# Block loads and VectorE block transposes for q and k, and w_in kept once in DRAM, in a fused attention, MoE and soft-MoE kernel

## The chip, the cores and the metric

The kernel runs on one core of one Trainium2 chip. The metric is the device time of one execution in microseconds. Three executions of the kernel before took 681.17, 681.69 and 682.29 us: a median of 681.69 us.

## The reference, cut to what matters

Three layers follow one another. q, k and v are float32 with 4 batches, 12 heads, 448 rows and 64 columns. The weights w_in and w_out come in as float64.

```python
scores = scale * np.matmul(q, k.transpose(0, 1, 3, 2))
scores = np.where(mask, -1000000000.0, scores)
attn = softmax(scores)
x = np.matmul(attn, v)                     # -> (4*448, 768)
h = x @ w_in                               # 768 -> 2048
g = h * np.clip(h + 3.0, 0.0, 6.0) / 6.0
x = g @ w_out                              # 2048 -> 768
logits = x @ phi                           # 32 slots
slot_input = softmax(logits, axis=0).T @ x
slot_out[e] = np.maximum(slot_input[e] @ w1[e], 0.0) @ w2[e]   # 8 experts
out = softmax(logits, axis=1) @ slot_out
```

## The kernel before, in words

**The stages.** The heads of a batch are taken in pairs, so there are 24 pairs (`attention(i)`, `i` from 0 to 23), six to a batch. After the six pairs of a batch come its 16 units of the middle layer (`ft` from 0 to 15), each a product of 128 columns of w_in with the 448 tokens of the batch. The units of one batch run between the pairs of the next, so that pairs and units alternate from the end of batch 0 on. After the last unit of batch 3 come the expert stage and the output, which stream w1 and w2 (named `in_moe_w_dram` in the profile, into `ring` tiles) from DRAM.

**The order of the work.** `Schedule` is a planner that runs when the kernel is built. Each step has an engine (or a choice of engines), a cost, the steps that it depends on, the buffers that it uses and a due time. `run` places the steps one after the other and so writes out the order of every engine's queue; the numbers in `TU` are its due times and weights. It decides, too, which engine takes a step that has a choice, and puts in filler matmuls (L385) where it sees TensorE idle. On the chip every engine then works through its own queue in that order and waits where an operand isn't there. All DMAs are issued on one queue, SP's (`dma`, L401).

**q and k of a pair.** Two DMAs each bring q and k into `qr` and `kr` (one buffer each) with 112 rows to a partition group. Four TensorE transposes each (L434) turn them into a PSUM tile `t`, of which there are two, shared with the units. ScalarE copies the tile into the first half of `qp` or `kp` (L404), rounded to fp32r, and VectorE subtracts that from the tile for the second half (L440). Products are then made of the three larger terms of (hi + lo) times (hi + lo). The scores are made first with hi alone (L457) in two halves that share one PSUM tile `ps`, VectorE takes the row maxima of each half (L472, L476), POOL or VectorE makes a diagonal matrix of them (L486 to L490), TensorE makes the transposed scores less the maxima (L507, L512), ScalarE the exponentials (L522), POOL cuts them at the diagonal (L530), in two steps, and TensorE multiplies by v (L545). The result is normalised (L556 to L558), turned (L566) and split into hi and lo (L404, L574) as `xp`.

**w_in of a unit.** The float64 bits of w_in are turned into float32 on the chip in batch 0 (`conv`, L587 to L599) and land in one of two `cx` tiles. That float32 tile is stored to DRAM as `wf_d`, split into hi and lo (ScalarE L682, VectorE L685 or POOL L687) in one of two `wpl` tiles, and the split pair is stored, too, as `wi_d`. Batches 1 and 2 load the split pair (768 KB) straight into `wpl`; batch 3 loads the float32 tile (384 KB) into `cx` and splits it again. A unit is 18 matmuls of 448 columns (L701), then L706 and L708 make g, four transposes (L715) turn it, and ScalarE stores it (L720, L722).

```python
if b == 0 or fin:                                       # L681: split on the chip
    e = sc.add("ACT", 0.84, ...)                        # L682
    wr = sc.any([("DVE", 1.0, ...), ("POOL", 2.0, ...)], [e], [cx, w], ps_)
elif not fin:                                           # L693: load the split pair
    wr = sc.load(0.79e6, ...dma(w.t.bitcast(F32), wi_d[ft])...)
```

## Time and profile before

| what | value |
|---|---|
| time, median of three | 681.69 us |
| time of the profiled execution | 680.19 us |
| its span | 678.4 us |
| PEld (weight loads, beside the matmuls) | 478.2 us, 70% |
| DVE (VectorE) | 329.7 us, 49% |
| ACT (ScalarE) | 261.4 us, 39% |
| POOL (GpSimd) | 96.5 us, 14% |
| DMA | 161.56 MB, 72.9% of 16 engines |
| granted clock of TensorE, mean | 0.956 |

The span is the time from the first to the last instruction of the profiled execution; some 1.8 us of its time lie around it. PE is the matmul side of TensorE. Busy shares are means over stages that differ: the first stage is attention of batch 0 beside the conversion of w_out, the middle ones are units and pairs, and the last is a stream of weights. The table of stretches among the rows below keeps them apart.

### The profile page before, as it was taken

The page shows a single profiled execution, that of the slowest core. Times are in us where ns is not written, and L with a number is a line of the kernel's source. Part 1 is how long each engine was busy: PE and PEld are TensorE (multiplying, and loading weights), DVE is VectorE, ACT ScalarE, POOL GpSimd, SP SyncE. Part 2 cuts the span into 40 slices and gives each one's busy share as a digit, 9 for nine tenths or more (in the row PEclk, how much of TensorE's full clock was granted, in tenths as well). Part 3 has the DMA queues.
Part 4 walks back from the last instruction along what each step waited for, and adds up shares of the span by engine and source line. Part 5 has one row for each costly group of instructions (what it writes and reads, how often), then busy time and mean ns, then how long its engine had stood idle before and what let it go on. Part 6 is the DMA issues. An engine that isn't in the chain of part 4 may idle for free.

```text
span 678.4 us, 15815 instructions
## 1 busy us (share of the span) xinstructions
PE 628.4 (93%) x6556; PEld 478.2 (70%) x6556; DVE 329.7 (49%) x814; ACT 261.4 (39%) x488; POOL 96.5 (14%) x197
## 2 busy tenths in 40 slices
PE   8798989999999999999999999999999999977474
PEld 6677868787888778888888688888698843522133
DVE  6886978888784534444335554323433333101101
ACT  2575566544544433323334332334344322201011
POOL 1332332325340011110001001000000000000000
PEclk7998999999999999999999999999999999996666
DMA  8989899989979833555445343335962399999997
GB/s 205 312 293 297 270 262 335 338 236 333 298 267 361 264 89 122 157 159 138 141 142 168 91 135 124 124 135 212 370 239 93 117 341 385 378 373 357 331 313 220
DMA packets 142615, 161.56 MB, mean 238 GB/s; under 512 B 71632, under 2 KB 113872, under 8 KB 142544
## 3 DMA queue, kind: packets, MB, share of 16 engines
q1 hardware_dynamic: 142544, 160.56, 72.9%
q8 instruction: 51, 0.84, 0.5%
q14 instruction: 20, 0.16, 0.1%
HBM read 129.86 MB, written 30.67 MB: 237 GB/s over the span
## 4 chain that ended last, share of the span: by engine, by line
PE 68%; DMA 13%; DVE 9%; SPq 3%; issue 2%; ACT 2%; POOL 0%; DVEq 0%; ACTq 0%; POOLq 0%
PE ph L701 19%; PE pl L701 13%; DMA ring<-in_moe_w_dram 7%; PE ps L507 5%; PE t L715 5%; DVE ps L472 4%; DMA raw<-in_moe_w_out_dram 3%; PE o L545 3%; SPq L401 3%; PE t L566 3%; PE ps L457 2%; PE t L434 2%; PE t L859 2%; PE ps L1025 2%; PE ph L730 2%
## 5 line engine op out<-in xcount | busy, mean ns | idle before, releaser
L701 PE MATMUL ph<-xp,wpl 128*128 128x448 f32 x720 | 157.0, 371 | 0.0
L701 PEld LDWEIGHTS ph<-xp,wpl 128*128 128x128 f32 x720 | 132.2, 188 | 15.2 <-ACT r L706 2.2
L701 PE MATMUL pl<-xp,wpl 128*128 128x448 f32 x432 | 94.2, 371 | 0.0
L701 PEld LDWEIGHTS pl<-xp,wpl 128*128 128x128 f32 x432 | 79.4, 188 | 9.0 <-issue 2.6
L472 DVE CUSTOM_DVE_ANT_0 ps<-ps,maskw 128x448 f32<-128x448 f32 (+3 forms) x144 | 61.7, 429 | 48.5 <-PE ps L457 38.6
L530 POOL TENSOR_SCALAR_AFFINE_SELECT s<-s 128x256 f32<-128x256 f32 x96 | 43.6, 478 | 232.9 <-ACT s L522 141.5
L706 ACT ACTIVATE r<-ph,three 128x448 f32<-128x448 f32 x40 | 25.5, 637 | 102.5 <-PE ph L701 102.5
L507 PE MATMUL ps<-qp,kp 64*64 64x64 f32 (+3 forms) x576 | 57.5, 306 | 3.8 <-ACT s L522 3.8
L522 ACT ACTIVATE s<-ps 128x896 f32<-128x896 f32 (+2 forms) x72 | 50.3, 734 | 25.9 <-PE ps L512 22.0
L708 DVE SCALAR_TENSOR_TENSOR g<-r,ph 128x448 f32<-128x448 f32 x40 | 24.7, 618 | 62.9 <-ACT r L706 62.9
L507 PEld LDWEIGHTS ps<-qp,kp 64*128 64x128 f32 (+1 forms) x576 | 42.1, 175 | 17.7 <-issue 6.6
L545 PE MATMUL o<-vr,s 128*64 128x65 f32 (+1 forms) x1536 | 53.6, 224 | 0.0
L545 PEld LDWEIGHTS o<-vr,s 128*64 128x64 f32 (+1 forms) x1536 | 48.6, 137 | 5.8 <-issue 3.8
L587 ACT ACTIVATE ca<-raw 128x768 f32<-128x768 f32 x32 | 29.3, 917 | 29.7 <-DMA raw<-in_moe_w_out_dram 10.0
L708 DVE SCALAR_TENSOR_TENSOR g<-r,pl 128x448 f32<-128x448 f32 x24 | 14.8, 617 | 50.8 <-ACT r L706 50.8
L720 ACT ACTIVATE gtok<-t 128x384 f32<-128x384 f32 x64 | 31.2, 487 | 19.2 <-PE t L715 19.0
L715 PE MATMUL t<-ident,g 128*128 128x128 f32 (+1 forms) x256 | 37.9, 279 | 0.2 <-DVE g L708 0.2
L706 ACT ACTIVATE r<-pl,three 128x448 f32<-128x448 f32 x24 | 15.3, 636 | 58.3 <-PE pl L701 58.3
L596 DVE SCALAR_TENSOR_TENSOR cw<-ca,cw 128x768 uint32<-128x768 uint32 x32 | 32.9, 1029 | 3.4 <-ACT ca L587 1.7
L1123 PE MATMUL o<-ring,wos 128*32 128x384 f32 (+1 forms) x256 | 22.5, 474 | 11.8 <-DMA ring<-in_moe_w_dram 11.8
L715 PEld LDWEIGHTS t<-ident,g 128*128 128x128 f32 (+1 forms) x256 | 26.9, 133 | 6.1 <-issue 1.5
L457 PE MATMUL ps<-kp,qp 64*128 64x448 f32 (+1 forms) x192 | 27.3, 344 | 4.1 <-DVE mc L472 3.0
(209 smaller groups left out, 827.1 us busy)
## 6 DMA issues: line engine op xcount, KB each, us to landing
ring<-in_moe_w_dram SPq DMA_DIRECT2D x45, 768.0 KB, 11.6
wpl<-wi_d SPq DMA_DIRECT2D x32, 768.0 KB, 4.2
raw<-in_moe_w_out_dram SPq DMA_DIRECT2D x16, 768.0 KB, 6.1
raw<-in_moe_w_in_dram SPq DMA_DIRECT2D x16, 768.0 KB, 7.4
wi_d<-wpl SPq DMA_DIRECT2D x16, 768.0 KB, 6.1
ring<-in_moe_w_dram SPq DMA_DIRECT2D x21, 512.0 KB, 8.0
wo_d<-gtok SPq DMA_DIRECT2D x16, 384.0 KB, 4.1
wf_d<-cx SPq DMA_DIRECT2D x16, 384.0 KB, 7.5
```

The lines of the kernel that those rows point to most:

```text
L457: nc.tensor.matmul(ps.t[:n, h, c:c + w], pl["q"].t[r, 0, q0:q0 + n], pl["k"].t[r, 0, 0:w], start=(t == part[0][0]), stop=adds, skip_group_ ...
L472: nc.vector.tensor_tensor_reduce(out=x, in0=x, in1=maskw[:n, 320 - q0:320 + n] if t else maskw[:n, 320:320 + n], scale=-1.0, scalar=3.0e38 ...
L507: nc.tensor.matmul(ps.t[:kn, h, col:col + n], pl["k"].t[r, x, q0:q0 + kn], pl["q"].t[r, y, q0:S], start=(c == 0 and col == 0), stop=False, ...
L522: nc.scalar.activation(out=o, in_=x, func=ACTF.Exp, scale=SCALE)
L530: nc.gpsimd.affine_select(out=x, in_=x, pattern=[[0, 2], [1, kn]], compare_op=ALU.is_ge, fill=0.0, base=0, channel_multiplier=-1)
L545: nc.tensor.matmul(o.t[64 * h:64 * h + 64, VD * j:VD * j + VD], s.t[:kn, h, c:c + 64], vr.t[:kn, h, t, :], start=(t == 0), stop=(t == ts[- ...
L596: e = sc.add("DVE", 1.04, lambda: nc.vector.scalar_tensor_tensor(out=cw.t, in0=ca.t.bitcast(U32), scalar=3, in1=cw.t, op0=ALU.logical_shif ...
L701: nc.tensor.matmul(h.t[:, :S], w.t[:, a, kk, :], x.t[:, c, kk, :], start=(n == 0), stop=(n == len(seq) - 1))
L706: rr = sc.add("ACT", 0.63, lambda h=h, r=r: nc.scalar.activation(out=r.t, in_=h.t[:, :S], func=ACTF.Relu, bias=three), [hh], [h, r], pr - ...
L708: gg = sc.add("DVE", 0.62, lambda h=h, r=r, g=g: nc.vector.scalar_tensor_tensor(out=g.t, in0=r.t, scalar=6.0, in1=h.t[:, :S], op0=ALU.min, ...
L715: nc.tensor.transpose(tp.t[:n, t * P:(t + 1) * P], g.t[:, t0:t0 + n], ident)
L720: nc.scalar.activation(out=gflat[:, :3 * DFF].rearrange("p (t f) -> p t f", f=DFF)[:, :, c], in_=v3[:, 0:3, :], func=ACTF.Copy)
```

## The change

q and k of pairs 6 to 23 (batches 1 to 3, `TU["DV"]` is 6) are no longer turned by TensorE. Four DMAs each bring them in as blocks of 32 rows by 32 columns, each row of a block 128 B long, so that 32-column groups of the two heads lie on partition groups of 32. One VectorE instruction turns every 32 by 32 block in place of the four TensorE transposes, from SBUF into one of two new SBUF tiles `tt`. The copy and the subtraction then read `tt`, and the subtraction may go to POOL. w_in is stored once, as float32 (`wi_d`, 384 KB a unit), and batches 1 to 3 all load that into `cx` and split it on the chip. The numbers of `TU` are others.

```diff
-        wf_d = [dram.tile([P, KD, P], F32, name=f"wf_d{i}") for i in range(KF)]
-        wi_d = [dram.tile([P, 2, KD, P], F32, name=f"wi_d{i}") for i in range(KF)]
+        wi_d = [dram.tile([P, KD, P], F32, name=f"wi_d{i}") for i in range(KF)]
...
-        many(atp, TU["Q"], "qr", [112, QR, 2, DH])
-        many(atp, TU["Q"], "kr", [112, QR, 2, DH])
+        many(atp, TU["Q"], "qr", [P, 512])
+        many(atp, TU["Q"], "kr", [P, 512])
+        many(atp, TU["TT"], "tt", [P, S])
...
+            blocks = i >= TU["DV"]
+
             def ld(buf, src):
                 for h in range(2):
-                    dma(buf.t[:, :, h, :], src[b, 2 * hp + h].rearrange("(r p) d -> p r d", r=QR))
+                    if not blocks:
+                        dma(buf.t[:112, :].rearrange("p (r h d) -> p r h d", r=QR, h=2)[:, :, h, :],
+                            src[b, 2 * hp + h].rearrange("(r p) d -> p r d", r=QR))
+                    for c in range(2 * blocks):
+                        r = 64 * h + 32 * c
+                        dma(buf.t[r:r + 32, :S].rearrange("p (n d) -> p n d", d=32),
+                            src[b, 2 * hp + h, :, 32 * c:32 * c + 32].rearrange("(n p) d -> p n d", p=32))
...
-                a = sc.add("PE", 0.5, tr, [l], [tp, buf, dst], p0)
+                if blocks:
+                    a = sc.add("DVE", 0.62, lambda tp=tp, buf=buf: nc.vector.transpose(tp.t, buf.t[:, :S]), [l], [tp, buf, dst], p0)
+                else:
+                    a = sc.add("PE", 0.5, tr, [l], [tp, buf, dst], p0)
...
-                los.append(sc.add("DVE", 0.61, lambda tp=tp, dst=dst: nc.vector.tensor_sub(
-                    dst.t[:, 1], tp.t[:, :S], dst.t[:, 0].bitcast(F32)), [c], [tp, dst], p0))
+                lo = [("DVE", 0.61, lambda tp=tp, dst=dst: nc.vector.tensor_sub(
+                    dst.t[:, 1], tp.t[:, :S], dst.t[:, 0].bitcast(F32)))]
+                if blocks:
+                    lo.append(("POOL", 1.2, lambda tp=tp, dst=dst: nc.gpsimd.tensor_sub(
+                        dst.t[:, 1], tp.t, dst.t[:, 0].bitcast(F32))))
+                los.append(sc.any(lo, [c], [tp, dst], p0 + (TU["LO"] if blocks else 0.0)))
...
-                if b == 0 or fin:
-                    cx = sc.buf("cx")
+                cx = sc.buf("cx")
...
-                    wf_stored[ft] = sc.load(0.39e6, lambda cx=cx, ft=ft: dma(wf_d[ft], cx.t), [cr], [cx], ps_)
-                elif fin:
-                    cr = sc.load(0.39e6, lambda cx=cx, ft=ft: dma(cx.t, wf_d[ft]), [wf_stored[ft]], [cx], ps_ - 10)
...
-                if b == 0:
-                    wi_stored[ft] = sc.load(
-                        0.79e6, lambda w=w, ft=ft: dma(wi_d[ft], w.t.bitcast(F32)), [wr], [w], ps_)
-                elif not fin:
-                    wr = sc.load(0.79e6, lambda w=w, ft=ft: dma(w.t.bitcast(F32), wi_d[ft]), [wi_stored[ft]], [w], ps_ - 10)
+                    wi_stored[ft] = sc.load(0.39e6, lambda cx=cx, ft=ft: dma(wi_d[ft], cx.t), [cr], [cx], ps_)
+                else:
+                    cr = sc.load(0.39e6, lambda cx=cx, ft=ft: dma(cx.t, wi_d[ft]), [wi_stored[ft]], [cx], ps_ - 10)
```

The planner writes a new order from this. Three places show it. The first is TensorE's queue in batch 1, from the fifth unit (L701, L708 in the change) to the sixth, with the two halves of a pair's scores (L457, L471), the attention sum of the pair before it (L545, L559) and the transposes of the next pair's q and k (L434). Before:

```order
438 L701 MATMUL pl<-xp_196,wpl_197 128x448 x18
439 L457 MATMUL ps_247<-kp_224,qp_222 128x448 x2
440 L457 MATMUL ps_247<-kp_224,qp_222 64x64 x2
441 L545 MATMUL o_248<-vr_217,s_225 64x65 x32
442 L457 MATMUL ps_247<-kp_224,qp_222 128x192 x2
443 L457 MATMUL ps_247<-kp_224,qp_222 128x320 x2
444 L434 MATMUL t_249<-ident,qr_215 128x112 x4
445 L434 MATMUL t_250<-ident,kr_216 128x112 x4
446 L701 MATMUL ph_244<-xp_196,wpl_198 128x448 x18
```

And of the change:

```order
420 L708 MATMUL pl<-xp_180,wpl_181 128x448 x18
421 L471 MATMUL ps_233<-kp_210,qp_208 128x448 x2
422 L471 MATMUL ps_233<-kp_210,qp_208 64x64 x2
423 L559 MATMUL o_234<-vr_203,s_211 64x65 x32
424 L471 MATMUL ps_233<-kp_210,qp_208 128x192 x2
425 L471 MATMUL ps_233<-kp_210,qp_208 128x320 x2
426 L722 MATMUL t_235<-ident,g_176 128x128 x3
427 L722 MATMUL t_235<-ident,g_176 64x128
428 L708 MATMUL ph_231<-xp_180,wpl_182 128x448 x18
```

The two rows of L434 are gone, and the transposes of a unit's g (L722) stand there, which stood behind the sixth unit before.

The second is VectorE's queue at the 19th pair: its q and k, beside the row maxima of the pair ahead of it (L472, L486, an instruction and its accumulator read in turn). Before:

```order
459 L708 SCALAR_TENSOR_TENSOR g_192<-r_193,pl 128x448
460 L574 TENSOR_TENSOR xp_195<-t_250,xp_195 128x448
461 L708 SCALAR_TENSOR_TENSOR g_188<-r_193,ph_244 128x448
462 L440 TENSOR_TENSOR qp_221<-t_250,qp_221 128x448
463 L472 ISA ps_247,mc_228<-ps_247,maskw 128x448
464 L472 ISA mc_228 128x1
```

And of the change:

```order
494 L697 TENSOR_TENSOR wpl_181<-cx_183,wpl_181 128x768
495 L715 SCALAR_TENSOR_TENSOR g_172<-r_177,ph_231 128x448
496 L444 STREAM_TRANSPOSE tt_202<-qr_199 128x448
497 L444 STREAM_TRANSPOSE tt_201<-kr_200 128x448
498 L450 TENSOR_TENSOR qp_207<-tt_202,qp_207 128x448
499 L450 TENSOR_TENSOR kp_209<-tt_201,kp_209 128x448
500 L486 ISA ps_233,mc_214<-ps_233,maskw 128x448
501 L486 ISA mc_214 128x1
```

The two block transposes (L444) and both subtractions (L450) stand ahead of the row maxima, with a split of w_in (L697) before them; before, one subtraction stood there, and the other after the second half of the maxima.

The third is POOL's queue at the 16th pair, in batch 2, with the cuts of the exponentials (L530, L544). Before:

```order
132 L490 TENSOR_TENSOR dg_232<-id_203,mc_228 128x448
133 L530 AFFINE_SELECT s_226<-s_226 128x2x128
134 L530 AFFINE_SELECT s_226<-s_226 64x2x64
135 L530 AFFINE_SELECT s_226<-s_226 128x2x128 x2
136 L486 COPY mc_227<-mc_227 128x7
```

And of the change:

```order
138 L699 TENSOR_TENSOR wpl_181<-cx_183,wpl_181 128x768
139 L544 AFFINE_SELECT s_212<-s_212 128x2x128
140 L544 AFFINE_SELECT s_212<-s_212 64x2x64
141 L699 TENSOR_TENSOR wpl_181<-cx_183,wpl_181 128x768
142 L544 AFFINE_SELECT s_212<-s_212 128x2x128 x2
143 L699 TENSOR_TENSOR wpl_182<-cx_184,wpl_182 128x768
```

A split of w_in (L699) stands between the two cuts of a pair's `s`. Such a split between two cuts stands at 12 places in the change, and at none before.

## Rows read from the trace of the kernel before

**Rows 1.** The page: span, and part 1, busy time of each engine
```profile
span 678.4 us, 15815 instructions
...
PE 628.4 (93%) x6556; PEld 478.2 (70%) x6556; DVE 329.7 (49%) x814; ACT 261.4 (39%) x488; POOL 96.5 (14%) x197
```

**Rows 2.** Windows by stage: stretch, length, busy time of each engine, clock, DMA share, GB/s
```profile
0.00:107.00 107.00, 94.33 (x1353) 75.62 (x1353) 84.53 (x161) 61.21 (x97) 32.52 (x64) 0.95 0.90 277
107.00:240.00 133.00, 130.80 (x1366) 108.79 (x1363) 98.05 (x229) 67.32 (x121) 36.96 (x58) 1.00 0.91 300
240.00:385.00 145.00, 143.44 (x1523) 116.97 (x1521) 64.23 (x210) 49.55 (x98) 17.94 (x53) 1.00 0.46 139
385.00:480.00 95.00, 94.51 (x898) 79.87 (x894) 36.02 (x103) 35.95 (x74) 7.26 (x21) 1.00 0.44 150
480.00:545.00 65.00, 65.00 (x373) 52.45 (x372) 22.27 (x33) 27.34 (x56) 0.00 (x0) 1.00 0.54 189
545.00:595.00 50.00, 47.08 (x571) 22.67 (x569) 13.63 (x61) 9.56 (x22) 1.80 (x1) 1.00 1.04 380
595.00:678.00 83.00, 53.20 (x498) 21.86 (x490) 11.00 (x22) 10.47 (x22) 0.00 (x0) 0.71 1.02 319
```

**Rows 3.** Windows of line L434 alone (q and k transposes): stretch, PE busy (count)
```profile
107.00:240.00 133.00, 7.67 (x56) 5.84 (x56) 1.00 0.91 300
240.00:385.00 145.00, 7.40 (x56) 5.62 (x56) 1.00 0.46 139
385.00:480.00 95.00, 2.14 (x16) 1.61 (x16) 1.00 0.44 150
```

**Rows 4.** Timeline of PE at three places: start, us, engine, line, tiles, count
```profile
135.57 0.60 PE L434 MATMUL t<-ident,kr 112*128 112x112 f32 x4
136.10 2.23 PE L545 MATMUL o<-vr,s 128*64 128x65 f32 x64
...
256.90 0.60 PE L434 MATMUL t<-ident,kr 112*128 112x112 f32 x4
257.34 0.60 PE L715 MATMUL t<-ident,g 128*128 128x128 f32 x4
...
274.16 0.60 PE L434 MATMUL t<-ident,qr 112*128 112x112 f32 x4
274.60 0.55 PE L434 MATMUL t<-ident,kr 112*128 112x112 f32 x4
274.92 0.46 PE L701 MATMUL ph<-xp,wpl 128*128 128x448 f32 x1
```

**Rows 5.** Groups of instructions by form: busy us, mean ns of one, idle before
```profile
L682 ACT ACTIVATE wpl<-cx 128x768 fp32r<-128x768 f32 x32 | 26.9, 841 | 2.1 <-DVE cx L599 1.9
...
L685 DVE TENSOR_TENSOR wpl<-cx,wpl 128x768 fp32r<-128x768 f32 x25 | 24.3, 970 | 10.1 <-ACT wpl L682 9.5
...
L440 DVE TENSOR_TENSOR qp<-t,qp 128x448 fp32r<-128x448 f32 x24 | 14.9, 620 | 20.3 <-ACT qp L404 20.2
...
L687 POOL TENSOR_TENSOR wpl<-cx,wpl 128x768 fp32r<-128x768 f32 x7 | 13.5, 1925 | 15.9 <-ACT wpl L682 15.9
...
L404 ACT ACTIVATE qp<-t 128x448 fp32r<-128x448 f32 x24 | 13.0, 543 | 22.6 <-PE t L434 22.3
```

**Rows 6.** Timeline of POOL and PE, a cut and the attention sum behind it
```profile
268.06 0.77 POOL L530 TENSOR_SCALAR_AFFINE_SELECT s<-s 128x256 f32<-128x256 f32 x2 [2.58 <-ACT s L522]
...
271.06 2.23 PE L545 MATMUL o<-vr,s 128*64 128x65 f32 x64
```

**Rows 7.** DMA issues from 240 to 385 us: KB each, us to landing
```profile
qr<-in_q_dram SPq DMA_DIRECT2D x14, 112.0 KB, 2.5
```

**Rows 8.** DMA from 2 to 9 us: packets, and their share of 16 engines
```profile
DMA packets 5233, 1.21 MB, mean 173 GB/s; under 512 B 5230, under 2 KB 5230, under 8 KB 5233
...
q1 hardware_dynamic: 5233, 1.21, 80.6%
```

**Rows 9.** Timeline of the DMA-issuing queue (SP)
```profile
238.21 0.87 SPq L401 DMA_DIRECT2D kr<-in_k_dram  x2
```

More of the change, by code (lines that the diff above doesn't have):

```diff
@@ L17 @@
 PSUM = bass.MemoryType.PSUM
[L20 removed]
+TU = {'PO': [0.0, -14.01, -18.7, -2.86], 'TO': [-7.42, -5.8, 41.18, 1.8], 'PB': 0.71, 'AB': -0.57, 'TB': 242.38, 'DUTY': 0.6, 'RINGS': [2, 4, 2, 3, 1, 6, 2, 3], 'LOOK': 0.28, 'FILL': 0.96, 'RAW': 3, 'CA': 1, 'CW': 1, 'S': 2, 'PAIR': 11.35, 'UNIT': 2.56, 'WP0': 31.11, 'WPS': 9.72, 'T0': 166.71, 'L0': 16.88, 'L1': 5.94, 'GP': 249.05, 'TP': 9.64, 'ZP': 104.14, 'UP': -2.06, 'P0': 15.72, 'NQ': 2, 'WAIT': 0.11, 'AHEAD': 2.19, 'LAT': 0.23, 'CX': 2, 'G': 5, 'R': 1, 'VR': 2, 'XT': 2, 'Q': 1, 'AS': 1.42, 'A1': -4.01, 'A2': 3.42, 'A3': 15.93, 'A4': -9.99, 'A5': 12.02, 'A6': 20.26, 'A7': 9.91, 'DG': 2, 'DV': 6, 'TT': 2, 'LO': 1.0, 'DA': 6}
 class Step:
@@ L426, in attention @@
             for nm, buf, src in (("q", qr, q), ("k", kr, k)):
-                l = sc.load(0.46e6, lambda buf=buf, src=src: ld(buf, src), [], [buf], p0 - 30, 2)
-                tp, dst = sc.buf("t"), sc.buf(nm + "p")
+                l = sc.load(0.46e6, lambda buf=buf, src=src: ld(buf, src), [], [buf], p0 - 30, 4 if blocks else 2)
+                tp, dst = sc.buf("tt" if blocks else "t"), sc.buf(nm + "p")
                 pl[nm] = dst
@@ L432, in tr @@
                     for r in range(QR):
-                        x = buf.t[:, r].rearrange("p h d -> p (h d)")
-                        nc.tensor.transpose(tp.t[:, 112 * r:112 * r + 112], x, ident[:112, :112])
-                a = sc.add("PE", 0.5, tr, [l], [tp, buf, dst], p0)
+                        nc.tensor.transpose(tp.t[:, 112 * r:112 * r + 112], buf.t[:112, P * r:P * r + P], ident[:112, :112])
+                if blocks:
+                    a = sc.add("DVE", 0.62, lambda tp=tp, buf=buf: nc.vector.transpose(tp.t, buf.t[:, :S]), [l], [tp, buf, dst], p0)
+                else:
+                    a = sc.add("PE", 0.5, tr, [l], [tp, buf, dst], p0)
                 a.weight = 0.3
@@ L658 @@
         T1 = 1e5
-        wi_stored, wf_stored = {}, {}
+        wi_stored = {}
         prev_u = None
@@ L677 @@
                     cr = conv(src, lambda cx=cx: cx.t, [cx], [], ps_, ft)
-                    wf_stored[ft] = sc.load(0.39e6, lambda cx=cx, ft=ft: dma(wf_d[ft], cx.t), [cr], [cx], ps_)
-                elif fin:
-                    cr = sc.load(0.39e6, lambda cx=cx, ft=ft: dma(cx.t, wf_d[ft]), [wf_stored[ft]], [cx], ps_ - 10)
-                if b == 0 or fin:
-                    e = sc.add("ACT", 0.84, lambda w=w, cx=cx: nc.scalar.activation(
-                        out=w.t[:, 0], in_=cx.t, func=ACTF.Copy), [cr], [cx, w], ps_)
-                    wr = sc.any([
-                        ("DVE", 1.0, lambda w=w, cx=cx: nc.vector.tensor_sub(
-                            w.t[:, 1], cx.t, w.t[:, 0].bitcast(F32))),
-                        ("POOL", 2.0, lambda w=w, cx=cx: nc.gpsimd.tensor_sub(
-                            w.t[:, 1], cx.t, w.t[:, 0].bitcast(F32))),
-                    ], [e], [cx, w], ps_)
-                if b == 0:
-                    wi_stored[ft] = sc.load(
-                        0.79e6, lambda w=w, ft=ft: dma(wi_d[ft], w.t.bitcast(F32)), [wr], [w], ps_)
-                elif not fin:
-                    wr = sc.load(0.79e6, lambda w=w, ft=ft: dma(w.t.bitcast(F32), wi_d[ft]), [wi_stored[ft]], [w], ps_ - 10)
+                    wi_stored[ft] = sc.load(0.39e6, lambda cx=cx, ft=ft: dma(wi_d[ft], cx.t), [cr], [cx], ps_)
+                else:
+                    cr = sc.load(0.39e6, lambda cx=cx, ft=ft: dma(cx.t, wi_d[ft]), [wi_stored[ft]], [cx], ps_ - 10)
+                e = sc.add("ACT", 0.84, lambda w=w, cx=cx: nc.scalar.activation(
+                    out=w.t[:, 0], in_=cx.t, func=ACTF.Copy), [cr], [cx, w], ps_)
+                wr = sc.any([
+                    ("DVE", 1.0, lambda w=w, cx=cx: nc.vector.tensor_sub(
+                        w.t[:, 1], cx.t, w.t[:, 0].bitcast(F32))),
+                    ("POOL", 2.0, lambda w=w, cx=cx: nc.gpsimd.tensor_sub(
+                        w.t[:, 1], cx.t, w.t[:, 0].bitcast(F32))),
+                ], [e], [cx, w], ps_)
                 h, r, g, x = sc.buf("h"), sc.buf("r"), sc.buf("g"), xb[b]
```

1 line of the change is left out of this document (removed).

## The prediction

> **What bounds the kernel now.** I read the table of busy time by engine first, then the windows by stage, then the timeline of TensorE (PE) inside the middle stage. The page has PE busy for 628.4 of 678.4 us [rows 1], but that is an average over stages with different limits, so the windows decide. From 0 to 107 us (attention of batch 0 beside the conversion of w_out) PE has 94.33 us of work and DMA a share of 0.90: a mixed stage, with 12.7 us of idle PE. From 107 to 480 us (units of the middle layer between the pairs of batches 1 to 3) PE is busy for 130.80 of 133, 143.44 of 145 and 94.51 of 95 us. That is 4.25 us of idle in 373, all at full clock, while VectorE has 198 us of work there, ScalarE 153 and POOL 62. From 480 to 545 us only units are left and PE is busy throughout. From 545 us on the DMA share is 1.02 to 1.04: the stream of expert weights sets the end, and it starts with the buffers that the last unit frees. All of this is in [rows 2]. So up to 545 us the time is the sum of what stands in PE's queue; every microsecond taken out of it before the last unit brings the weight stream, and so the end, forward by one. The weight stream itself isn't touched.
>
> **What is removed from PE.** Eighteen pairs lose two sets of four transposes: 36 sets, 144 matmuls. What a set costs is not the length of its row but the distance to the next start, since matmuls overlap. In the timeline [rows 4] a set starts at 135.57 and the next work at 136.10, which is 0.53 us; then 256.90 to 257.34, 0.44; 274.16 to 274.60, 0.44; 274.60 to 274.92, 0.32. The mean is 0.43, and 36 times that is **15.6 us**. From below, every set is worth the smallest, 0.32: 11.5 us. From above I take the busy time: 7.67 + 7.40 + 2.14 = 17.21 us for 128 of these matmuls [rows 3], so 19.4 for 144. I take 15.6, since the distance between starts is what the queue pays.
>
> **What of that is not gained.** By the order before, five of the 36 sets stand between the two halves of a pair's scores (the one at 135.57 is of this kind, ahead of the attention sum at 136.10 [rows 4]). The second half waits there for the row maxima of the first, because both use the one PSUM tile. Without the set, PE waits in its place. I count all five as lost: 5 times 0.43, **+2.2 us**. The other 31 stand behind the second half, as in the piece of order shown, with a unit or its transposes behind them, which wait for nothing of this pair.
>
> **What is added on VectorE, ScalarE and POOL.** No row shows a block transpose. The nearest is the 448-column subtraction, 620 ns [rows 5]. I take 0.62 us, with half and twice that as bounds: 36 times 0.62 is 22 us (11 to 45). The order gives VectorE 7 more splits of w_in at 970 ns (6.8 us) and 9 fewer subtractions (5.6 us less), and six diagonal steps that POOL did (each one 448-column instruction and four tiny copies, about 1 us by estimate from the same row). In all that is some 30 us, of which nearly all falls between 107 and 480: 228 of about 360 us, 63% against 53% before; with the upper bound 70%. ScalarE gets 32 more splits at 841 ns, 26.9 us: 180 of 360. POOL goes from 7 splits to 32 at 1925 ns [rows 5], 48 us, and does 9 subtractions (1.1 us each, by columns from that same row): it ends near 110 of 360. The copies into qp and kp keep their number and, I take it, their 543 ns. None of the three becomes full, so this work is hidden by PE's; what it costs is waits where a queue holds an instruction that PE needs. The busy time of VectorE and ScalarE together grows by a sixth; a sixth of the 4.25 us of idle is **+0.7 us**. The bounds are far apart: all 4.25 us of idle could go, and the rivals give the other side.
>
> **The waits.** In VectorE's queue the block transposes stand ahead of the row maxima of the pair before. If the blocks of q or k land late, maxima, g of the units and everything behind them wait, and PE with them. What covers this is the lead: 17 pairs in 373 us is one every 21.9 us; the single buffer is free for the next load as soon as it is turned, and a load lands 2.5 us after its issue [rows 7].
>
> **DMA and its queue.** From 2 to 9 us nearly all packets are of 256 B, and 5233 of them took 80.6% of 16 engines [rows 8]: 0.806 x 16 x 7 us / 5233 = 17.3 ns each. A packet of 128 B costs between half of that and the same. A pair now needs 3584 of these for q and k in place of 1792 of 256 B: between nothing and 1.9 us more of all 16 engines, at most 35 us over 18 pairs. I take the upper end. Against it go 16 stores of 768 KB and half of 32 loads of 768 KB, 25 MB, some 70 us at the 340 to 380 GB/s of the last stages [rows 2]. DMA is relieved most from 107 to 240, where its share is 0.91. SP issues 72 more loads and 16 fewer stores; two issues take 0.87 us [rows 9], so it works 24 us more in 373 and the last quarter of a tensor is issued 0.9 us later. Both are covered by the 21.9 us above. I cost DMA at nothing.
>
> The Trainium skill speaks against such a load (VectorE: DVE Perf Modes, "The three transpose paths"): a plain DMA that transposes by access-pattern strides is given as 19 times slower than the DMA's own transpose when the innermost stride is large. By that rule the sum would not hold, and the time is among the rivals. Here the DMA moves whole runs of 128 B and VectorE turns the blocks, and no run so far shows such a load.
>
> **First stage and tail.** Before the first unit the change touches pairs 6 and 7 only, whose sets are counted; the conversion of w_out stays, in another order. I take 0, with 4 us either way, a third of the idle there. The tail from 545 us needs the same bytes from the same number of buffers: 0.
>
> **The sum.** 680.19 (the profiled execution: 678.4 of span and 1.8 around it) - 15.6 + 2.2 + 0.7 = 667.5 us. The median of the runs is 1.5 us above that execution, so I forecast **669.0 us**. With the bounds of the removed sets and of the first stage it is 661 to 676.
>
> **Rivals.**
> *Slower: splits in POOL's queue hold the attention sums.* At 12 places a split of w_in stands between the two cuts of a pair, and the attention sum waits for both. Now the second cut starts at 268.06, takes 0.77, and the sum starts at 271.06 [rows 6]: a slack of 2.2 us, against 1.93 for a split. For it: the slack is hardly larger than the split, and the split itself waits for its load and for ScalarE. Against it: a unit of 3.9 us usually stands ahead of the sum. If each place cost a whole split, that is 12 x 1.93 = 23 us: 692 us. It decides from 1.2 us a place, which takes the time to 683.
> *Little gained: each unit waits for its split.* In batches 1 and 2, 32 units used to get their weights by one load; now load, ScalarE and VectorE or POOL follow each other. Batch 3 does this already, with units packed closest, and PE is busy for all of 480 to 545 us [rows 2], which speaks against it; that batch 3 has no pairs on these engines speaks for it. At 0.3 us a unit it is 9.6 us: 678.6. From 0.4 us nothing is left that can be measured.
> *More gained.* DMA relief takes the 4.25 us of idle in the middle and the first stage gains 4 us: 669.0 - 0.7 - 4.25 - 4 = 660.
> *The blocks come late.* If a load took 19 times the 2.5 us [rows 7], 47.5 us against a lead of 21.9, each pair would be 25.6 us late: 18 x 25.6 = 461, some 1130 us. For a time above 683 it takes 0.8 us a pair. This is the skill's rule from above; the packet price of [rows 8] speaks against it.
> *The change doesn't do what it says:* the order rules that out for the sets; they are gone from PE's queue, and the filler matmuls in it go only from 62 to 65.
>
> **How the numbers follow.** Less than 0.2% (1.4 us) can't be told from no change here. The forecast gets 0.66, little gained 0.15, the splits on POOL 0.10, more gained 0.07, the late blocks 0.02. Faster by over 0.2%: 0.66 + 0.07 + 0.11 of the second case = 0.84. Within 0.2%: 0.04 of the second case and 0.02 of the third, 0.06. Slower: 0.08 + 0.02 = 0.10. The range runs from 660 to 680: outside lie 0.12 for the two slow cases, about 0.04 of the gain beyond 660 and 0.03 of the second case, 0.19.
>
> **What would show it.** Right: in the windows the first unit starts near 107 us as before and the last ends some 13 us ahead of 545, with PE as full as before; L701's matmuls unchanged; block transposes near 0.6 us; DMA share from 107 to 240 well under 0.91. Wrong: waits of PE for POOL's cuts or VectorE's maxima of more than 10 us in all, VectorE waiting for loads of qr or kr, or a first stage that moved by more than 4 us.

## The result, and the profile after

| | before | after |
|---|---|---|
| median (runs) | 681.97 us (681.17 to 682.29, 4) | 674.93 us (670.64 to 676.61, 4) |
| profiled execution | 680.19 us | 670.64 us |
| ratio, 95% interval | | 0.9889 [0.9842, 0.9936] |

The forecast was 669.0 us within 660 to 680. The kernel became faster and the time lies in the range, but of the 12.7 us forecast 7.0 came, and the execution that was profiled is 4.3 us below the median of its kernel. Where single executions of a version fell into a slower state of the chip, the medians and ratios below are of the others. The page of after, span and busy time of each engine, answers to [rows 1]:

```profile
span 668.9 us, 15717 instructions
...
PE 616.1 (92%) x6418; PEld 465.7 (70%) x6418; DVE 374.0 (56%) x881; ACT 281.5 (42%) x517; POOL 151.2 (23%) x201
```

TensorE's busy time fell by 12.3 us (628.4 to 616.1), while VectorE works 44 us more, ScalarE 20 and POOL 55. As in the prediction, the windows decide. I cut the span at the first and at the last matmul of the units (L701, now L708). Windows of before, with the columns of [rows 2]: first stage, stretch of the units, rest.

```profile
0.00:107.40 107.40, 94.73 (x1362) 75.79 (x1362) 84.93 (x162) 61.61 (x97) 32.52 (x64) 0.95 0.90 277
107.40:542.25 434.85, 430.60 (x4123) 356.58 (x4120) 219.54 (x569) 178.37 (x346) 62.16 (x132) 1.00 0.60 198
542.25:678.40 136.15, 103.03 (x1078) 45.87 (x1076) 25.25 (x84) 21.43 (x46) 1.80 (x1) 0.82 1.02 336
```

The same three windows of after:

```profile
0.00:109.15 109.15, 94.50 (x1355) 74.89 (x1355) 87.84 (x160) 58.99 (x95) 39.60 (x73) 0.95 0.86 251
109.15:530.75 421.60, 417.90 (x3990) 343.64 (x3987) 260.34 (x637) 201.59 (x379) 109.75 (x127) 1.00 0.53 150
530.75:668.90 138.15, 103.70 (x1078) 47.12 (x1076) 25.83 (x85) 20.90 (x45) 1.80 (x1) 0.81 0.99 331
```

In this pair of executions the stretch lost 13.25 us, the first stage grew by 1.75 and the rest by 2.0, together 9.5. PE is as full as before in the stretch: 3.70 us of idle against 4.25. The groups that answer to [rows 5], with the new block transposes (columns as there):

```profile
L694 ACT ACTIVATE wpl<-cx 128x768 fp32r<-128x768 f32 x64 | 53.6, 838 | 11.9 <-PE ph L708 6.0 <-DVE cx L613 5.6
L697 DVE TENSOR_TENSOR wpl<-cx,wpl 128x768 fp32r<-128x768 f32 x32 | 30.7, 958 | 15.2 <-ACT wpl L694 13.3
L699 POOL TENSOR_TENSOR wpl<-cx,wpl 128x768 fp32r<-128x768 f32 x32 | 62.3, 1946 | 88.9 <-ACT wpl L694 83.8 <-PE t L580 5.1
L444 DVE STREAM_TRANSPOSE tt<-qr 128x448 f32<-128x448 f32 x18 | 11.4, 636 | 0.0
L444 DVE STREAM_TRANSPOSE tt<-kr 128x448 f32<-128x448 f32 x18 | 10.8, 602 | 0.0
L404 ACT ACTIVATE qp<-tt 128x448 fp32r<-128x448 f32 x18 | 10.3, 573 | 1.7 <-DVE tt L444 1.7
L450 DVE TENSOR_TENSOR kp<-tt,kp 128x448 fp32r<-128x448 f32 x14 | 10.6, 756 | 2.6 <-ACT kp L404 2.5
L450 DVE TENSOR_TENSOR qp<-tt,qp 128x448 fp32r<-128x448 f32 x13 | 10.4, 800 | 9.8 <-ACT qp L404 9.7
```

The block transpose costs what was taken for it, and it never waited for its load in the trace (0.0 of idle before it). Subtractions that read the turned block from tt took longer on average than those from PSUM (756 and 800 ns against 620); the last section shows when.

What PE waited for in the stretch of the units after the change (engine, tile, line, releaser, us in total, times, longest; the five longest):

```profile
PE ph L708 <- POOL wpl L699: 1.1, 1, 1.1
PE ps L471 <- DVE mc L486: 0.8, 2, 0.5
PE ps L471 <- DVE rc L570: 0.5, 1, 0.5
PE pl L737 <- DVE g L715: 0.5, 1, 0.5
PE ps L526 <- POOL dg L504: 0.4, 1, 0.4
```

So by its size the middle went as forecast, and the question is the first stage. There PE has one wait that before hadn't. Timeline of VectorE after the change, from 74.9 to 82 us (start, us, engine, line, operation, tiles, count, idle and releaser):

```profile
74.92 0.60 DVE L444 STREAM_TRANSPOSE tt<-kr 128x448 f32<-128x448 f32 x1
80.01 0.56 DVE L604 TENSOR_SCALAR cw<-raw 128x768 uint32<-128x768 uint32 x1 [4.50 <-DMA raw<-in_moe_w_out_dram]
80.49 0.62 DVE L450 TENSOR_TENSOR qp<-tt,qp 128x448 fp32r<-128x448 f32 x1
81.03 1.28 DVE L490 TENSOR_REDUCE mc<-ps 128x2 f32<-128x896 f32 x2
```

and of PE behind it:

```profile
82.36 0.36 PE L471 MATMUL ps<-kp,qp 64*128 64x192 f32 x2 [3.97 <-DVE mc L490]
```

VectorE waits for a piece of w_out that is late; the row maxima stand behind that conversion in its queue, and the second half of a pair's scores waits for the maxima. The queue that issues the transfers shows what was busy ahead of it (SP, start and length of each group of issues):

```profile
62.35 3.02 SPq L401 DMA_DIRECT2D qr<-in_q_dram  x4
65.47 3.90 SPq L401 DMA_DIRECT2D kr<-in_k_dram  x4
69.47 2.38 SPq L401 DMA_DIRECT2D vr<-in_v_dram  x3
71.94 0.54 SPq L401 DMA_DIRECT2D wo_d<-gtok  x1
72.58 0.38 SPq L401 DMA_DIRECT2D raw<-in_moe_w_out_dram  x1
...
75.02 6.26 SPq L401 DMA_DIRECT2D qr<-in_q_dram  x4
```

Two issues of kr took 0.87 us in [rows 9]; here eight of q and k take 6.92, and the next four alone 6.26. Theory 1 for the shortfall: the block loads of the first pairs hold SP, the issuing queue, while w_out is loaded. Theory 2: the constants, which were changed with the code, set another order. Theory 3: the work added on VectorE and ScalarE. Beside these stands the main question: is it PE's queue, the saved bytes or the constants that gave the gain?

### The profile page after: what moved, and what is told of

Read it like the earlier page. It is cut to its first block, busy times and chain, and to the rows that moved or that the text cites. A ratio compares the mean times of both kernels' runs of the same rounds, so it can differ in the third digit from the quotient of the medians.

```text
span 668.9 us, 15717 instructions
## 1 busy us (share of the span) xinstructions
PE 616.1 (92%) x6418; PEld 465.7 (70%) x6418; DVE 374.0 (56%) x881; ACT 281.5 (42%) x517; POOL 151.2 (23%) x201
## 5 line engine op out<-in xcount | busy, mean ns | idle before, releaser
L708 PE MATMUL ph<-xp,wpl 128*128 128x448 f32 x828 | 180.7, 371 | 1.5 <-POOL wpl L699 1.1
L708 PEld LDWEIGHTS ph<-xp,wpl 128*128 128x128 f32 x828 | 152.1, 188 | 19.5 <-ACT r L713 2.9
L544 POOL TENSOR_SCALAR_AFFINE_SELECT s<-s 128x256 f32<-128x256 f32 x96 | 50.9, 553 | 146.0 <-ACT s L536 137.6
L699 POOL TENSOR_TENSOR wpl<-cx,wpl 128x768 fp32r<-128x768 f32 x32 | 62.3, 1946 | 88.9 <-ACT wpl L694 83.8
L713 ACT ACTIVATE r<-ph,three 128x448 f32<-128x448 f32 x46 | 29.1, 633 | 105.0 <-PE ph L708 105.0
L486 DVE CUSTOM_DVE_ANT_0 ps<-ps,maskw 128x448 f32<-128x448 f32 (+3 forms) x144 | 61.8, 429 | 19.9 <-PE ps L471 15.9
L708 PE MATMUL pl<-xp,wpl 128*128 128x448 f32 x324 | 71.2, 373 | 0.0
L715 DVE SCALAR_TENSOR_TENSOR g<-r,ph 128x448 f32<-128x448 f32 x46 | 28.4, 618 | 65.5 <-ACT r L713 62.0
L708 PEld LDWEIGHTS pl<-xp,wpl 128*128 128x128 f32 x324 | 59.6, 188 | 6.4 <-issue 1.1
L521 PE MATMUL ps<-qp,kp 64*64 64x64 f32 (+3 forms) x576 | 57.3, 305 | 2.7 <-ACT s L536 2.7
L694 ACT ACTIVATE wpl<-cx 128x768 fp32r<-128x768 f32 x64 | 53.6, 838 | 11.9 <-PE ph L708 6.0
L521 PEld LDWEIGHTS ps<-qp,kp 64*128 64x128 f32 (+1 forms) x576 | 41.7, 174 | 20.8 <-issue 9.4
L559 PE MATMUL o<-vr,s 128*64 128x65 f32 (+1 forms) x1536 | 53.6, 224 | 0.0
L559 PEld LDWEIGHTS o<-vr,s 128*64 128x64 f32 (+1 forms) x1536 | 48.6, 137 | 5.6 <-issue 3.8
L697 DVE TENSOR_TENSOR wpl<-cx,wpl 128x768 fp32r<-128x768 f32 x32 | 30.7, 958 | 15.2 <-ACT wpl L694 13.3
L722 PE MATMUL t<-ident,g 128*128 128x128 f32 (+1 forms) x256 | 38.0, 280 | 0.0
L471 PE MATMUL ps<-kp,qp 64*128 64x448 f32 (+1 forms) x192 | 27.0, 340 | 7.1 <-DVE mc L490 4.6
```

The costliest lines, as they stand in the source:

```text
L486: nc.vector.tensor_tensor_reduce(out=x, in0=x, in1=maskw[:n, 320 - q0:320 + n] if t else maskw[:n, 320:320 + n], scale=-1.0, scalar=3.0e38 ...
L521: nc.tensor.matmul(ps.t[:kn, h, col:col + n], pl["k"].t[r, x, q0:q0 + kn], pl["q"].t[r, y, q0:S], start=(c == 0 and col == 0), stop=False, ...
L544: nc.gpsimd.affine_select(out=x, in_=x, pattern=[[0, 2], [1, kn]], compare_op=ALU.is_ge, fill=0.0, base=0, channel_multiplier=-1)
L559: nc.tensor.matmul(o.t[64 * h:64 * h + 64, VD * j:VD * j + VD], s.t[:kn, h, c:c + 64], vr.t[:kn, h, t, :], start=(t == 0), stop=(t == ts[- ...
L694: e = sc.add("ACT", 0.84, lambda w=w, cx=cx: nc.scalar.activation(out=w.t[:, 0], in_=cx.t, func=ACTF.Copy), [cr], [cx, w], ps_)
L697: ("DVE", 1.0, lambda w=w, cx=cx: nc.vector.tensor_sub(w.t[:, 1], cx.t, w.t[:, 0].bitcast(F32))),
```

## The experiments

Each traced run is cut at the first and the last matmul of its units. "First stage by median" is the median less 1.8 us around the span, less the stretch and the rest of that trace: an estimate, made because one execution's first stage says little (first experiment). It is a remainder, so anything that differs between the traced execution and the median is counted in it. The ratio is taken against executions of before made beside each version, so it isn't the quotient of two medians of this table. Where 156 of the matmuls of L521 stand ahead of the first unit it is the same work; in four versions (marked *) 168 do: half a pair's second scores moved there, 1.2 us by the timeline of after (107.59 to 108.80), out of the stretch.

| kernel | median, us | ratio to before, 95% | stretch (PE idle) | rest | first stage by median |
|---|---|---|---|---|---|
| before, its two traces | 681.97 | 1 | 434.85 (4.25), 434.26 (3.77) | 136.2, 136.4 | 109.3 |
| after, its two traces * | 674.93, 674.96 | 0.9889, 0.9905 | 421.60 (3.70), 421.90 (3.85) | 138.2, 137.8 | 113.4 |
| constants alone | 685.13 | 1.0031 [1.0005, 1.0057] | 434.99 (3.29) | 136.2 | 112.1 |
| no blocks | 682.57 | 1.0000 [0.9971, 1.0029] | 432.82 (1.40) | 138.4 | 109.5 |
| dummies put back * | 689.69 | 1.0146 [1.0098, 1.0193] | 435.76 (3.03) | 136.6 | 115.6 |
| constants of before | 676.63 | 0.9914 [0.9888, 0.9940] | 427.45 (5.10) | 137.2 | 110.2 |
| three constants of before * | 675.78 | 0.9894 [0.9867, 0.9921] | 421.29 (3.60) | 138.1 | 114.6 |
| blocks from pair 8 | 673.79 | 0.9891 [0.9861, 0.9921] | 424.24 (4.22) | 137.6 | 110.1 |
| blocks from pair 12 | 672.63 | 0.9856 [0.9827, 0.9885] | 423.04 (1.28) | 137.3 | 110.5 |
| the same again | 673.78 | 0.9901 [0.9867, 0.9936] | 422.98 (1.28) | 138.8 | 110.2 |
| blocks for pairs 6 to 11 * | 687.79 | 1.0121 [1.0067, 1.0175] | 433.17 (5.11) | 138.7 | 114.1 |
| loads of 6 to 11 cut in four | 677.03 | 0.9937 [0.9908, 0.9967] | 424.08 (2.36) | 137.1 | 114.1 |

**Both kernels again.** The kernel after, unaltered:

> The changed kernel again, unaltered, for its spread and a second trace. If the order on the queues makes the late first stage (theory), the trace has TensorE waiting 3 to 5 us for VectorE's row maxima near 78 us again, behind a late load of w_out, and the first unit starts at 108.5 to 110 us. If that wait was an accident of one execution (rival), it is under 1.5 us here and the first unit starts before 108. The median should lie between 672 and 677 us.

Median 674.96 us, ratio 0.9905 [0.9870, 0.9940]. The wait near 78 us came again and was longer:

```profile
85.74 0.53 PE L471 MATMUL ps<-kp,qp 64*128 64x192 f32 x2 [5.29 <-DVE mc L490]
```

It is no accident of one execution. The span is 4.3 us longer than in the first trace, and the first unit starts 4.32 us later (113.47); the stretch (421.90) and the rest (137.83) are those of the first trace within 0.3. Its first stage, with the columns of the windows above:

```profile
0.00:113.47 113.47, 94.62 (x1355) 75.15 (x1355) 87.85 (x160) 59.06 (x95) 39.52 (x73) 0.95 0.81 242
```

The kernel before, also unaltered:

> The kernel before once more, for a second trace. If its executions differ in the first stage alone, as those of the change do, its stretch from the first to the last unit is 434 to 436 us again, what follows the last unit 135.5 to 137 us, and the first unit's start moves with the span: some 107 us at a span of 678, 110 to 111 at 682. If the spread comes from the end instead, the first unit starts at 107 to 108 us at any span.

Median 683.36 us, ratio 1.0009 [0.9973, 1.0045]. Its windows at a span of 685.5 us:

```profile
0.00:114.82 114.82, 100.73 (x1361) 80.39 (x1361) 84.36 (x162) 61.15 (x97) 31.98 (x64) 0.90 0.86 256
114.82:549.08 434.26, 430.49 (x4123) 356.69 (x4120) 220.24 (x569) 177.69 (x346) 63.43 (x132) 1.00 0.61 199
549.08:685.50 136.42, 104.69 (x1078) 46.42 (x1076) 25.27 (x84) 21.35 (x46) 1.80 (x1) 0.80 1.02 335
```

The span grew by 7.1 us and the first unit's start by 7.4. In both kernels the executions differ in the first stage and almost nowhere else, but not in the same way. In the change PE has the same 94.5 us of work at the same granted clock (0.95), and the 4.3 us are idle time. In before PE needs 100.73 us for the work that took 94.73, at a granted clock of 0.90 against 0.95, and that is 6.0 of the 7.4 us: not a wait for a load. From 20 to 30 us the clock was 0.53 there, close to the lower of its two levels (1.2 GHz), against 1.00 in the first trace; in the ten us ahead PE had been busy for 7.5 and 6.9 us. So a single trace says much of the stretch and little of the first stage, and there medians have to be compared.

**The constants alone**, in the code of before (its table of constants replaced by that of the change):

> The code of before with the constants of the change: neither block transposes nor the new handling of w_in. Theory (only the transposes taken out of TensorE's queue pay): not faster than before, 680 to 690 us, TensorE as full from the first to the last unit as before. Rival (the new constants made the gain): 677 us or less.

685.13 us, 1.0031 [1.0005, 1.0057]: the constants bring nothing by themselves, if anything a small loss, and that ahead of the first unit (111.9 us in the trace, 112.1 by the median).

**No blocks:** the change with

```
-'DV': 6
+'DV': 24
```

> The changed kernel with every pair's q and k turned by TensorE: of the change only w_in as float32 and the constants stay. Theory: the bytes saved were hidden, so no gain, 680 to 690 us; the DMA share from 100 to 240 us falls below that of before (0.91) and TensorE's time from the first to the last unit stays within 3 us of the 431.3 us of before. Rival (relief of the DMA engines made part of the gain): 676 us or less, with that stretch 427 us or shorter.

682.57 us, 1.0000 [0.9971, 1.0029]. The DMA share over the stretch fell from 0.62 (constants alone) to 0.48:

```profile
112.07:544.89 432.82, 431.42 (x4144) 357.55 (x4142) 245.53 (x609) 200.07 (x380) 77.58 (x124) 1.00 0.48 143
```

PE's idle time fell by 1.9 us with it (3.29 to 1.40), so the relief may have reached PE, but what follows the last unit is 2.2 us longer than with the constants alone and the total is that of before. The expectations count the stretch to the start of the last unit (431.3 before, 418 after); to its last matmul, as here, it is 434.85 and 421.60. Together with the constants, handling w_in otherwise brings nothing against before, as forecast. Against the constants alone, its nearest relative, it gains 2.6 us, with intervals that overlap, so whether the saved bytes are worth that isn't settled. From this version to the change it is another 7.6 us: the whole gain comes with the blocks.

**Dummies put back on TensorE**, in the step that turns the attention result:

```
 def xtr():
+    for n in range(2 * QR * blocks):
+        r = 112 * (n % QR)
+        nc.tensor.transpose(xq.t[:, r:r + 112], maskw[:112, 0:P], ident[:112, :112])
```

> The changed kernel, with the eight transposes of each of the pairs 6 to 23 put back on TensorE as dummies just ahead of the transposes of the attention result; blocks, splits and order stay as they are, and what the dummies write is overwritten. Theory (what leaves TensorE's queue comes off the time one for one): 36 sets x 0.43 us = 15 us more, less what falls into waits: 684 to 692 us, and the stretch from the first to the last unit grows from 418 to 429 to 434 us. Rival (TensorE isn't what sets this stretch any more, but VectorE, ScalarE or the loads): under 678 us.

689.69 us, 1.0146 [1.0098, 1.0193], and the stretch:

```profile
109.96:545.72 435.76, 432.73 (x4135) 357.99 (x4131) 260.36 (x637) 202.55 (x379) 109.61 (x127) 1.00 0.52 145
```

Against after, PE's busy time is 14.83 us longer, the stretch 14.16 and the median 14.8. With every block, split and wait of the change in place, 144 matmuls cost 0.41 us of PE for each four, and the stretch grows by nearly as much. In the stretch the work moved to the other engines doesn't set the time; PE's queue does. The median agrees in part by luck: by the table the first stage is 2.2 us longer and the rest 1.6 shorter, and neither was touched.

**Which pairs pay.** Blocks for 12 of the 18 pairs (`'DV': 12` in place of 6), run twice:

> The change with blocks for 12 of the 18 pairs (12 to 23). Theory (one for one): two thirds of the 11.2 us between the version without blocks and the change, so the stretch from the first to the last unit takes 424 to 427 us and the median is 676 to 681. Rival (VectorE's or ScalarE's load matters, so that the first pairs taken off pay most and the last ones nothing): under 423 us in the stretch.

> Blocks from pair 12 on once more, with more rounds, since it came out below the change (672.6 against 675 us). If that is real, the median is 671 to 674 us and the stretch from the first to the last unit 422.5 to 423.5 us with under 1.5 us of idle on TensorE; if it was the spread, 674 to 677 us.

672.63 and 673.78 us: the stretch is as short as after's plus the moved 1.2 (422.98 against 422.8), though only 24 sets are gone instead of 36. Here is its stretch:

```profile
112.50:535.54 423.04, 421.76 (x4042) 347.79 (x4040) 257.08 (x637) 200.84 (x380) 97.63 (x120) 1.00 0.52 146
```

Against the version without blocks 9.66 us of PE's busy time are gone for 24 sets, 0.40 a set, and 9.78 us of the stretch: paid in full. The complement, blocks for pairs 6 to 11 alone:

```
-blocks = i >= TU["DV"]
+blocks = TU["DV"] <= i < 12
```

> The complement of the run with blocks from pair 12 on: blocks for pairs 6 to 11 alone, TensorE turns the others. Theory (the pairs that run beside the first stage and the conversion of w_in pay nothing, because VectorE is 0.87 to 0.91 busy there and TensorE's idle time grows by what its queue loses, and because their loads stand in SP's queue in the first stage): the stretch from the first to the last unit is within 2 us of the 432.8 us of the version without blocks, and the median is 681 to 685 us. Rival (each pair pays the same 0.8 us wherever it stands, and the change lost its part elsewhere): 12 sets x 0.40 us less than 682.6, so 677 to 679 us.

687.79 us, 1.0121 [1.0067, 1.0175], slower than before and 5.2 us above the version without blocks. Its stretch:

```profile
114.35:547.52 433.17, 428.06 (x4090) 353.13 (x4087) 245.10 (x603) 201.31 (x379) 96.07 (x137) 1.00 0.49 145
```

PE has 3.4 us less work there than without blocks (2.2 when the moved 1.2 is taken off), but 5.1 us of idle instead of 1.4, and the first stage by median is 4.6 us later; of those 1.2 is the moved work; the stretch, that work put back, is 1.6 us longer instead of shorter. I had expected that these six pairs pay nothing; alone they cost. So a third of the change costs when it stands alone. On top of the other two thirds it brings nothing; by the medians it costs 1.2 to 2.3 us, which the overlapping intervals don't settle.

**Why the first stage is late.** The code of the change with all constants of before (theory 2; the table of before, with DV 6, TT 2 and LO 1.0 added):

> The code of the change with the constants of before. Theory now (the 14.2 us came back when the sets were put back, and the code of before with the new constants starts its first unit 4.5 us late, at 111.9 us, without any block load): the new constants cost the first stage 2 to 6 us and the blocks cost it nothing, so here the first unit starts at 106 to 109 us, the stretch to the last unit takes 420 to 425 us, and the median is 667 to 671 us, below the change's 675. Rival (the block loads hold SP's queue while w_out is loaded): the first unit starts at 109 to 113 us again and the median is 673 to 677.

676.63 us: the first unit did start early by the median (110.2), but the stretch became 427.45, with 5.10 us of idle and 32 filler matmuls, so nothing is gained. Three constants of before alone:

```
-'WP0': 31.11, 'WPS': 9.72, 'P0': 15.72
+'WP0': 17.76, 'WPS': 10.66, 'P0': 12.1
```

> The change with three constants of before, those that place the conversion of w_out and the pairs of batch 0 (WP0, WPS, P0). Theory (the first stage is late because the conversion of w_out starts 13 us later in the order): first unit at 106 to 109.5 us, no wait of TensorE over 2.5 us between 70 and 92 us, 668 to 672 us. Rival (it isn't these three): first unit after 109.5, 673 to 678 us.

675.78 us; the first unit at 115.2 us and a wait of 5.1 us near 78 us. The expectation of theory 2 failed: it isn't those three. Blocks from pair 8 on, which takes the block loads of pairs 6 and 7 out of the first stage but these pairs' sets with them (`'DV': 8`; theory 1 was the rival by then):

> The change with blocks from pair 8 on: pairs 6 and 7, whose loads are issued between 62 and 85 us, are loaded and turned as before. Rival (those loads' issue time on SP makes the late load of w_out): VectorE's longest wait for w_out near 78 us falls under 2 us, the first unit starts at 105 to 108 us, and the median is 670 to 673. Theory (constants): the first unit starts at 110 to 113 us, and the four sets on TensorE again cost up to 1.7 us more: 674 to 678 us.

673.79 us, between the two expectations. VectorE's wait for w_out near 78 us fell to 1.9 us and the first stage by median to 110.1, but PE still waited 2.7 us there, for the exponentials of another pair. This left load and work mixed, since with a block both change. The last run separates them: blocks from pair 12 on, and pairs 6 to 11 loaded in rows and turned by PE, but each load cut in two.

```
-dma(... rearrange("p (r h d) -> p r h d", r=QR, h=2)[:, :, h, :],
-    src[b, 2 * hp + h].rearrange("(r p) d -> p r d", r=QR))
+n = 1 + (6 <= i < 12)
+for c in range(0 if blocks else n):
+    z = slice(64 // n * c, 64 // n * (c + 1))
+    dma(... rearrange("p (r h d) -> p r h d", r=QR, h=2)[:, :, h, z],
+        src[b, 2 * hp + h].rearrange("(r p) d -> p r d", r=QR)[:, :, z])
```

> The version with blocks from pair 12 on, in which pairs 6 to 11 are still loaded in rows and turned by TensorE, but each of their loads is cut in two halves of 32 columns: four issues and packets of 128 B for a tensor, as with blocks, and nothing else changes on any engine. Theory (the form of the load is what makes the first stage late: issue time on SP and small packets while w_out is loaded): the first unit starts some 3 us later by the medians and the median is 675 to 678 us, against 672.6 and 673.8. Rival (it is the work on VectorE and ScalarE, or the order that follows from it): 672 to 674.5 us.

677.03 us, 0.9937 [0.9908, 0.9967], 3.3 to 4.4 us above the two runs without the cut (2.5 to 5.5 by the ratios). The interval overlaps with that of the second of these, but eleven of its twelve executions lie above the longest of their ten (675.0 us). Order and work are the same on every engine; in SP's queue only the added issues differ. The SP queue in the run with the cut:

```profile
66.66 2.61 SPq L401 DMA_DIRECT2D qr<-in_q_dram  x4
69.37 4.09 SPq L401 DMA_DIRECT2D kr<-in_k_dram  x4
...
76.59 0.54 SPq L401 DMA_DIRECT2D raw<-in_moe_w_out_dram  x1
...
79.87 5.16 SPq L401 DMA_DIRECT2D qr<-in_q_dram  x4
85.13 4.92 SPq L401 DMA_DIRECT2D kr<-in_k_dram  x4
```

and in the second run without it:

```profile
65.56 1.03 SPq L401 DMA_DIRECT2D qr<-in_q_dram  x2
66.68 1.72 SPq L401 DMA_DIRECT2D kr<-in_k_dram  x2
...
72.55 0.54 SPq L401 DMA_DIRECT2D raw<-in_moe_w_out_dram  x1
...
78.60 1.60 SPq L401 DMA_DIRECT2D qr<-in_q_dram  x2
80.29 2.17 SPq L401 DMA_DIRECT2D kr<-in_k_dram  x2
```

The form of the load by itself delays the first stage, by 3.7 us by the medians (114.1 against 110.3), and the stretch by 1.1. In the traces PE is idle for 16.8 us of the first stage with the cut, and for 14.2 and 14.9 without it. Theory 1 holds as far as these runs go, and theory 3 isn't needed for it, since VectorE and ScalarE do the same work in both. The path differs from that of the change, though: PE's long wait here is 4.5 us for ScalarE's exponentials (2.8 and 1.2 without the cut), not for the row maxima. Whether it is the issue time on SP or the small packets in the DMA engines, both of which come with the cut, the traces tell in part. The first load of w_out behind these q and k was issued 9.9 us after the group's start with the cut, and 7.0 and 8.8 us after it in the two runs without. From its issue to its landing it took 5.7 us, against 5.4 and 5.2. So it comes late mainly because it is issued late; why SP's own issues take longer stays open. Nor is it the load alone: with the constants of before the same block loads came with a first stage of 110.2 by the median, and the new constants without any block with 112.1 (109.3 before), so the order counts too.

## Why the prediction was right, and where it was off

**What bounds the kernel: right from the first unit to the last.** PE's queue set the time of that stretch, and a microsecond out of it, or back in, was nearly a microsecond: 9.78 us for the 24 sets of pairs 12 to 23 taken out, 14.16 for 36 put in. That is why the sign was right at 0.84. All of after's gain is in the stretch: 12.8 us between the means of two traces each. That this is the 12.7 us of the sum is luck: 1.2 us of it is work that moved ahead of the first unit, 1.7 is there without any block, and the blocks' own part is 9.9.

**The 15.6 us removed: the price slightly too high, the count much too high.** I took 0.43 us from four distances between starts. The runs gave 0.40 (blocks from pair 12) and 0.41 (dummies); 36 sets are 14.4 to 14.8 instead of 15.6. But of the blocks' 9.9 us the 24 sets of pairs 12 to 23 alone pay 9.8. The twelve of pairs 6 to 11, 5.2 us of the sum, pay almost nothing: four stand ahead of the first unit, and what the other eight take from PE's queue came back as idle time.

**Sets between score halves: wrong, without harm.** All five were counted as lost, +2.2. PE's waits of this kind (L471 for the maxima of L486; before, L457 for L472) went from 2.7 us in six to 0.8 in two. The new order has other work there, which is read from the order of the changed kernel, not from that of before. Before:

```profile
PE ps L457 <- DVE mc L472: 2.7, 6, 0.6
```

**VectorE, ScalarE, POOL: right.** Taken 0.62 us for a block, measured 602 and 636 ns. ScalarE got 23 us more in the stretch (27 forecast), POOL ended at 109.75 us there ("near 110"). VectorE got 41 instead of 30: the subtractions from tt took some 0.16 us longer each (27 of them, about 4 us), which I hadn't priced. Another 5 came with the constants alone (224.51 against 219.54). It was covered in the end, as was the 30 ns more of each copy.

**The idle that the fuller engines cost: too small, and misplaced.** +0.7 was spread over the whole middle. Against the version without blocks PE's idle rose by 2.3 us (against before it fell by 0.2, by the means of two traces), and of after's 3.70 us 2.93 lie between 109 and 227 us, beside the conversion of w_in:

```profile
109.15:227.00 117.85, 114.92 (x1196) 94.51 (x1192) 99.58 (x216) 66.59 (x118) 57.50 (x59) 1.00 0.79 220
227.00:385.00 158.00, 157.69 (x1694) 128.06 (x1692) 97.61 (x283) 72.96 (x140) 40.64 (x54) 1.00 0.42 97
385.00:468.20 83.20, 83.10 (x758) 70.26 (x754) 41.59 (x107) 36.53 (x70) 11.61 (x16) 1.00 0.40 133
```

I had spread VectorE's load over the middle (63%); it is 84% in the first of these windows and 62% and 50% in the others. The averaging that I warned of between stages I did within one. That VectorE's share makes the idle time isn't shown, though: with blocks from pair 12 on it is busy for 82% of the like window (109.14 to 224.60 us of the second run), and PE is idle there for 0.73 us. In the last two windows PE is idle for 0.4 us in 241, and there blocks pay in full.

**DMA and its queue at nothing: the step that failed.** I reckoned 24 us more on SP over 373 us and covered the later issue of "the last quarter of a tensor" by a lead of 21.9 us a pair. From the first unit on that held: the loads of q and k landed 2.2 and 2.3 us after issue between 240 and 385 us (2.5 in [rows 7], larger pieces), and the transposes didn't wait. But pairs 6, 7 and 8 are loaded before the first unit, where no lead helps the others in SP's queue: w_out's loads stand behind them. "Two issues take 0.87 us" was the price of the old load; two of these took 0.86 to 0.98 us also in the first stage of before, at 66 and 79 us (1.80 at 55), but four of the new took 2.9 to 6.7 there. (The bytes saved, held to be worth some 70 us at 340 to 380 GB/s, were misread, too: the last stages moved 380 and 319 GB/s in [rows 2]. That changes nothing here.)

**First stage 0 with 4 us either way: mis-sized.** By medians it is 4.1 us later, of which 1.2 is moved work. The four sets of pairs 6 and 7 were counted at full price though they stand ahead of the first unit, in a stage where PE was idle for 12.7 us: 1.6 us that the stretch couldn't give. By the table the shortfall of 5.7 us stands outside the stretch: +4.1 (first stage), -12.8 (stretch), +1.7 (rest) is -7.0. That this closes says nothing, since the first stage by median is a remainder.

**The tail at 0:** it came out 1.7 us longer, and it is 136.6 to 138.8 in all versions with w_in as float32 against 136.2 to 136.4 with it as a pair. Why stays open. The last term, the 1.5 us between the profiled execution and the median, doesn't carry over: for the kernel after it was 4.3.

**The rivals.** *Splits on POOL hold PE* happened at one place, 1.1 us, not at twelve. *Each unit waits for its split* didn't: PE is busy for 62.18 of the last 62.55 us of the units and for nearly all of the two windows before. *More gained* may have been half right on the DMA relief (1.9 us of idle gone without blocks), but the rest of the span took it back. *The blocks come late* didn't happen: 2.2 us to landing, for pieces of 56 KB, against 2.5 for the loads in rows, of 112 KB. The rule of the Trainium skill (VectorE: DVE Perf Modes, "The three transpose paths") gives 19 times for a DMA that transposes by its access pattern where the innermost stride at the destination is large; here whole runs of 128 B are moved, so no run tests that rule. The harm came to other loads that shared the queue.

The best version is the one with blocks from pair 12 on, 672.63 and 673.78 us: below before without doubt (both intervals end under 0.994), and 1.2 to 2.3 us below the change's medians, which overlapping intervals don't settle.

## What to carry to other kernels

Ask of each part of a change in which stage it lands, and price it with a row of that stage: the same edit paid 0.4 us a set in the later pairs, and alone in the first third of them it cost 5 us. Those stand in the first stage, where DMA was 0.82 busy in that run, and beside the conversion of w_in. A load in finer pieces is paid by whoever stands behind it in the issuing queue, so look for that queue's next entries, not only for the load's own consumer. And a term proved for the whole should be tested by halves: the run with the first third of the change alone showed that it doesn't pay.
